# Transposing the last four token tiles by DMA, and moving query projections and evacuations forward, in a fused adaLN transformer block

## The chip, the cores and the metric

The kernel runs on one core of one Trainium2 chip. The metric is the device time of one execution in microseconds (us); lower is better. Kernels are compared in the same rounds on the same chip.

The engines are called PE (matrix multiplies; PEld is its weight loads), ACT (activation functions), DVE (vector work), POOL, and SP, which here issues the DMA transfers.

## The reference, cut to what matters

```python
mod = (_silu(c) @ w_mod).reshape(c.shape[0], 6, 1, -1)       # shift, scale, gate, twice
h = _layernorm(x) * (1 + ca) + sa                            # x: 1 x 2048 x 1024
x = x + ga * _A_ref(h, wq, wk, wv, wo)   # 32 query heads of 32, ONE key and value head
h = _layernorm(x) * (1 + cb) + sb
x = x + gb * _B_ref(h, w1, w3, w2)       # silu(h@w1) * (h@w3) @ w2, F = 3584
```

There are 2048 tokens, so 16 token tiles of 128. A "head group" is four query heads; there are eight. Every head needs a softmax over 2048 x 2048 scores. Those exponentials are ACT's main work: 1024 instructions, which start 0.92 us apart (median) when they follow one another.

## The kernel before

The program does not issue its instructions by hand. It adds nodes to a graph, each with an engine, a modelled duration, a priority (`prio`, lower goes first) and, for PE, the PSUM banks that it may use. At build time a list scheduler turns the graph into a fixed order for each engine. The program then holds one list for each engine, with waits on semaphores in it. So a change of priorities is a change of five orders.

Query block 0 (256 queries) starts while the first norm is still running, so this head of the kernel has much to arrange:

```python
def tr(t0, nt, allow=None):              # four token tiles: 32 PE transposes, 8 copies out of PSUM
    G.chain = 3
    ln_transpose(nt, t0, lambda c: HT[:, c, t0 * P:(t0 + nt) * P], ..., EV[t0 // 4], ...)
    G.chain = 0
...
def vproj(tb, allow=None):               # values of 512 tokens: 32 products of 128 x 32
    def vmm(e, b, i):
        tt, c = i // NC, i % NC
        return e.matmul(b[:, tt * 32:(tt + 1) * 32], HT[:, c, tb * 512 + tt * P:tb * 512 + (tt + 1) * P],
                        WKS[:, 1, c, :], start=c == 0, stop=c == NC - 1)
    ...
# the head, in the order in which the nodes are added
kproj(0, 256, (2, 3, 4, 5, 6, 7))        # keys; banks 2 to 7 are those of the scores
qproj(0, 256, 0, (2, 3, 4, 5, 6, 7), prio=1)
kproj(256, 256, (2, 3, 4, 5, 6, 7))
kproj(512, 512, (1,))
...
qproj(0, 256, 1, (0, 1))                 # queries of head group 1
vproj(0, (0, 1))
vproj(1, (0, 1))
for f in range(2, HEAD):
    qproj(0, 256, f, (0, 1))
tr(8, 4, (0, 1))
for t in range(12, 16):
    ln(t)
kproj(1024, 512, (0, 1))
tr(12, 4, (0, 1))
kproj(1536, 512, (0, 1))
for tb in range(2, NTB):
    vproj(tb, (0, 1))
...
wo_load = dma(lambda e: e.dma_start(WO[:], wo_in.rearrange("(c p) f -> p c f", p=P)), "wo", writes=["WO"],
              clear=[("WQR", k) for k in range(3)], nbytes=D * D * 2, after=xl)     # 2 MB
...
def warm(b, k):                          # PE work without a use, meant to hold the clock up (e5 and e6 test it)
    def f(e):
        for _ in range(k):
            r = e.matmul(PB[b][:, 0:P], IDENT[:], IDENT[:], start=True, stop=True, skip_group_check=True)
```

A score group is eight PE products that write the score banks; two exponentials on ACT read them.

The softmax here doesn't subtract the row's maximum and nothing guards it: scores larger than these inputs give would overflow.

## Time and profile before

| what | value | view |
|---|---|---|
| time | 1160.13 us, median of 3 (1158.57 to 1160.46) | runs |
| span of the profiled execution | 1158.1 us | page |
| busy PE, ACT | 97%, 89% | page |
| first and last exponential start | 29.2 and 1046.6 us | timeline |
| start of the last exponential to the end | 111.5 us, nearly PE alone | timeline |
| ACT waits for scores, 26 to 110 us | 11.7 us, longest 5.6 | waits |

From the first exponential to the last, ACT and PE are both nearly full. An exponential that starts 1 us earlier is worth up to 1 us, if nothing takes it back later and if the PE work left after the last exponential doesn't grow. So two quantities are followed below: the *lead* (how much earlier the n-th exponential starts than in the kernel before) and the *tail* (from the start of the last exponential to the end).

The page of the kernel before. The first line is the span, then the granted PE clock in tenths for 40 equal slices (29 us each), then two of the DMA queues.

```profile
span 1158.1 us, 35702 instructions
...
PEclk8899999999989999999999999999999999999999
...
q1 hardware_dynamic: 383184, 208.69, 64.5%
q8 instruction: 125, 2.05, 0.8%
```

The waits of the kernel before: ACT from 26 to 110 us, then one line of PE's from 20 to 110 us. Columns: total us, how often, longest.

```profile
engine line waited for: us in total, times, longest us
ACT UREG L925 <- PE SP L915: 11.7, 9, 5.6
...
PE PB L637 <- issue: 1.4, 1, 1.4
```

The timeline of the kernel before around its longest ACT wait. Columns: start, duration, engine, line, operation, tiles, count, and in brackets the idle time before it and what ended it.

```profile
57.75 0.37 SPq L813 DMA_DIRECT2D WO<-in_A_wo_dram  x1
...
59.67 1.05 PE L658 MATMUL PB<-HREG,WREG 128*128 128x256 bf16 x8
...
60.76 0.48 DVE L661 TENSOR_SCALAR QT<-PB,BIA 128x256 bf16<-128x256 f32 x1 [0.22 <-PE PB L658]
61.41 0.40 PE L915 MATMUL SP<-QT,KT 32*128 32x256 bf16 x8
...
61.86 14.38 ACT L925 ACTIVATE UREG<-SP 128x1024 bf16<-128x1024 f32 x15 [5.57 <-PE SP L915]
```

The fourth head group's query projection ran at 59.67 us, behind transposes and value products. Its scores at 61.41 us ended 5.57 us of ACT's idleness. The change aims at this wait.

The table by stretches of the kernel before. After the length come each engine's busy us, then the granted PE clock, the share of the DMA engines' time, and GB/s.

```profile
core 0: us, PE busy (x) PEld busy (x) DVE busy (x) ACT busy (x) POOL busy (x), PEclk, DMA share, GB/s
...
18.00:26.00 8.00, 7.41 (x132) 6.45 (x132) 2.55 (x5) 5.25 (x11) 0.42 (x1) 0.57 1.07 369
...
40.00:50.00 10.00, 8.42 (x156) 5.31 (x160) 8.31 (x27) 7.95 (x10) 4.89 (x12) 0.71 0.29 84
50.00:60.00 10.00, 8.40 (x203) 6.60 (x204) 7.97 (x25) 6.30 (x7) 0.18 (x1) 1.00 0.47 123
60.00:70.00 10.00, 10.00 (x194) 5.82 (x192) 3.64 (x9) 8.03 (x9) 0.00 (x0) 1.00 0.98 335
...
320.00:340.00 20.00, 11.53 (x232) 5.73 (x225) 15.55 (x26) 18.81 (x21) 1.70 (x2) 0.74 0.50 131
```

The clock fell twice in the head (0.57 and 0.71), and PE lost 8.5 of 20 us in a hole near 320 us.

### The profile page before, as it was taken

The page shows a single profiled execution, that of the slowest core. Times are in us where ns is not written, and L with a number is a line of the kernel's source. Part 1 is how long each engine was busy: PE and PEld are TensorE (multiplying, and loading weights), DVE is VectorE, ACT ScalarE, POOL GpSimd, SP SyncE. Part 2 cuts the span into 40 slices and gives each one's busy share as a digit, 9 for nine tenths or more (in the row PEclk, how much of TensorE's full clock was granted, in tenths as well). Part 3 has the DMA queues.
Part 4 walks back from the last instruction along what each step waited for, and adds up shares of the span by engine and source line. Part 5 has one row for each costly group of instructions (what it writes and reads, how often), then busy time and mean ns, then how long its engine had stood idle before and what let it go on. Part 6 is the DMA issues. An engine that isn't in the chain of part 4 may idle for free.

```text
span 1158.1 us, 35702 instructions
## 1 busy us (share of the span) xinstructions
PE 1122.6 (97%) x15918; PEld 767.1 (66%) x15918; DVE 984.7 (85%) x1498; ACT 1027.6 (89%) x1170; POOL 43.5 (4%) x86
## 2 busy tenths in 40 slices
PE   7799998999979999999999999999999999999998
PEld 6564444776646766777577766776677766777887
DVE  5837889999888999899999998999989999997452
ACT  5789999999999999999999999999999999992110
POOL 3200001000000001000100001000100010000000
PEclk8899999999989999999999999999999999999999
DMA  9337005956546565856496567766586649756996
GB/s 331 113 129 220 19 2 127 275 169 178 166 122 190 169 193 149 248 170 192 119 279 196 159 177 194 226 169 174 152 252 181 185 122 258 204 152 192 284 291 160
DMA packets 385417, 211.10 MB, mean 182 GB/s; under 512 B 21744, under 2 KB 376048, under 8 KB 385264
## 3 DMA queue, kind: packets, MB, share of 16 engines
q1 hardware_dynamic: 383184, 208.69, 64.5%
q8 instruction: 125, 2.05, 0.8%
q10 hardware_dynamic: 2080, 0.13, 0.1%
q14 instruction: 28, 0.23, 0.1%
HBM read 201.46 MB, written 4.19 MB: 178 GB/s over the span
## 4 chain that ended last, share of the span: by engine, by line
PE 92%; ACT 3%; DVE 3%; DMA 1%; SPq 1%; issue 0%; POOL 0%; DVEq 0%
PE PB L1141 33%; PE PB L1175 16%; PE SP L915 14%; PE PB L975 11%; PE PB L1107 5%; PE PB L658 4%; PE SP L1141 3%; ACT UREG L925 3%; PE SP L1175 2%; PE PB L1002 2%; DMA UREG<-in_w_mod_dram 1%; PE PB L637 1%; PE PB L838 0%; PE SP L1107 0%; DVE WO L850 0%
## 5 line engine op out<-in xcount | busy, mean ns | idle before, releaser
L925 ACT ACTIVATE UREG<-SP 128x1024 bf16<-128x1024 f32 x1024 | 968.6, 1075 | 18.8 <-PE SP L915 16.4
L948 DVE TENSOR_TENSOR UREG<-UREG 128x2048 bf16<-128x2048 bf16 x240 | 292.8, 1220 | 12.8 <-ACT UREG L925 10.8
L915 PE MATMUL SP<-QT,KT 32*128 32x256 bf16 x4096 | 204.8, 274 | 16.0 <-ACT UREG L925 15.0
L1141 PE MATMUL PB<-QT,WREG 128*128 128x256 bf16 x1648 | 207.4, 274 | 1.8 <-DVE DSB L1026 1.6
L1141 PEld LDWEIGHTS PB<-QT,WREG 128*128 128x128 bf16 x1648 | 150.1, 98 | 46.8 <-issue 31.2
L942 DVE TENSOR_TENSOR UREG<-UREG 128x2048 bf16<-128x2048 bf16 x120 | 146.4, 1220 | 11.5 <-PE PB L1002 6.4
L915 PEld LDWEIGHTS SP<-QT,KT 32*128 32x128 bf16 x4096 | 61.2, 93 | 138.6 <-ACT UREG L925 79.6
L1141 PE MATMUL PB<-QT,HREG 128*128 128x256 bf16 x1056 | 133.7, 274 | 0.8 <-DVE DSB L1026 0.8
L975 PE MATMUL PB<-UREG,V 128*32 128x256 bf16 x4032 | 132.2, 277 | 1.7 <-DVE QT L610 0.9
L975 PEld LDWEIGHTS PB<-UREG,V 128*32 128x32 bf16 x4032 | 99.3, 98 | 27.5 <-issue 17.9
L1141 PEld LDWEIGHTS PB<-QT,HREG 128*128 128x128 bf16 x1056 | 96.1, 98 | 29.7 <-issue 19.6
L1175 PE MATMUL PB<-WREG,HREG 128*128 128x256 bf16 x812 | 101.2, 273 | 0.0
L1175 PEld LDWEIGHTS PB<-WREG,HREG 128*128 128x128 bf16 x812 | 75.3, 98 | 20.4 <-issue 11.4
L1175 PE MATMUL PB<-HREG 128*128 128x256 bf16 x532 | 67.8, 274 | 0.0
L1141 PE MATMUL PB<-QT,X 128*128 128x256 bf16 x528 | 67.8, 274 | 0.0
L658 PE MATMUL PB<-HREG,WREG 128*128 128x512 bf16 (+1 forms) x312 | 64.1, 343 | 0.3 <-DVE DSB L1026 0.3
L957 DVE TENSOR_TENSOR UREG<-UREG 128x2048 bf16<-128x2048 bf16 x52 | 63.4, 1220 | 0.5
L1150 ACT ACTIVATE GSB<-GSB 128x512 bf16<-128x512 bf16 x56 | 38.8, 693 | 27.5 <-DVE GSB L1148 27.5
L1014 DVE COPY XN<-PB 128x256 f32<-128x256 f32 x63 | 26.6, 422 | 39.6 <-PE PB L1002 39.3
L1175 PEld LDWEIGHTS PB<-HREG 128*128 128x128 bf16 x532 | 49.2, 98 | 14.3 <-issue 8.0
L1107 PE MATMUL PB<-WO,QT 128*128 128x512 bf16 x232 | 57.6, 381 | 0.2 <-DVE QT L661 0.2
L1141 PEld LDWEIGHTS PB<-QT,X 128*128 128x128 bf16 x528 | 48.2, 98 | 14.3 <-issue 9.3
(139 smaller groups left out, 1031.9 us busy)
## 6 DMA issues: line engine op xcount, KB each, us to landing
WREG<-in_B_w_dram SPq DMA_DIRECT2D x112, 512.0 KB, 5.1
HREG<-in_B_w_dram SPq DMA_DIRECT2D x74, 512.0 KB, 5.2
WREG<-in_B_w_dram SPq DMA_DIRECT2D x33, 896.0 KB, 5.1
X<-in_B_w_dram SPq DMA_DIRECT2D x38, 512.0 KB, 5.1
HREG<-in_B_w_dram SPq DMA_DIRECT2D x21, 896.0 KB, 5.2
X<-in_B_w_dram SPq DMA_DIRECT2D x10, 896.0 KB, 5.1
X<-in_A_x_dram SPq DMA_DIRECT2D x32, 256.0 KB, 5.0
WREG<-in_w_mod_dram SPq DMA_DIRECT2D x16, 512.0 KB, 4.7
```

What stands on the lines that cost most here:

```text
L658: g = mm_group(NC, lambda e, b, c: e.matmul(b[:, 0:n], WQ[:, c, f * P:(f + 1) * P], HT[:, c, sl], start=c == 0, stop=c == NC - 1), lambda ...
L915: r = e.matmul(SP[:, b, o:o + qn], KT[32 * gg:32 * gg + 32, kts[j] * P:(kts[j] + 1) * P], QT[32 * gg:32 * gg + 32, f, q0:q0 + qn], start=T ...
L925: G.add("act", lambda e, u=u, h0=h0, n=n, b0=b0, nb=nb: e.activation(U[:, u, h0 * W:(h0 + n) * W].rearrange("p (b w) -> p b w", b=nb), SP[ ...
L942: G.add("dve", lambda e, tr=tr, u=u, fu=first_u: e.tensor_tensor(TR[:, tr, 0:4 * W], U[:, fu, 0:4 * W], U[:, u, 0:4 * W], ALU.add), reads= ...
L948: G.add("dve", lambda e, tr=tr, u=u: e.tensor_tensor(TR[:, tr, 0:4 * W], TR[:, tr, 0:4 * W], U[:, u, 0:4 * W], ALU.add), reads=[("TR", tr) ...
L957: G.add("dve", lambda e, ta=ta, tb=tb: e.tensor_tensor(TR[:, ta, 0:4 * W], TR[:, ta, 0:4 * W], TR[:, tb, 0:4 * W], ALU.add), reads=[("TR", ...
L975: r = e.matmul(PB[g.bank][32 * gg:32 * gg + 32, 0:qn], V[:, kt, :], U[:, pu, (gg * npk + j) * qn:(gg * npk + j + 1) * qn], start=w0 + n == ...
L1014: G.add("dve", lambda e, g=g, f=f: e.tensor_copy(ASB[:, f % 4, 0:qn], PB[g.bank][:, 0:qn]), writes=[("ASB", f % 4), ("XN", 2 + f % 4 // 2) ...
L1107: g = mm_group(NC, lambda e, b, f, t=t, h=h: e.matmul(b, QT[:, f, t * P:(t + 1) * P], WO[:, f, h * 512:(h + 1) * 512], start=f == 0, stop= ...
L1141: return e.matmul(b[:, j * qn:(j + 1) * qn], w13[:, w, c, j * P:(j + 1) * P], QT[:, c, q0:q0 + qn], start=c == 0, stop=c == NC - 1)
L1150: G.add("act", lambda e, b=b: e.activation(TB[b], GS[b], ACT.Tanh, scale=0.5), reads=[("GS", b)], writes=[("TB", b)], clear=alias("TB") if ...
L1175: G.add("pe", lambda e, g=g, j=j, fc=fc, hf=hf, first=first, w2s=w2s: e.matmul(PB[g.bank][:, j * 256:(j + 1) * 256], HHT[:, hf * NH + fc, ...
```

## The change

The intent was to take away ACT's waits in the head. Four query projections go ahead of values, evacuations of queries and values go ahead of norms on DVE, and the last four tiles (12 to 15) are transposed by DMA. The diff, cut to its core:

```diff
-              writes=[("V", tb)], groups=[(g, "r")], dur=dve_t(128), prio=1)
+              writes=[("V", tb)], groups=[(g, "r")], dur=dve_t(128), prio=-4)
...
-              writes=qkeys(f, t0, n), groups=[(g, "r")], dur=dve_t(n), prio=-5 if t0 == f == 0 else 1)
+              writes=qkeys(f, t0, n), groups=[(g, "r")], dur=dve_t(n), prio=-5 if t0 == 0 and f < HEAD else 1)
...
+    DMAT = range(12, 16)
-    EV = (("act",), ("act",), ("dve",), ("dve",))
+    EV = (("act",), ("act", "dve"), ("dve",), ("dve",))
...
+        if t in DMAT:
+            lastt[:] = [dma(lambda e: e.dma_start_transpose(HT[:, :, t * P:(t + 1) * P], xnt(t)), ("ht", t),
+                reads=[("XN", t)] + xnk(t), writes=[...], nbytes=P * D * 2 * 2)]
...
-    kproj(512, 512, (1,))
+    kproj(512, 512, (6, 7))
...
-    qproj(0, 256, 1, (0, 1))
+    qproj(0, 256, 1, (0, 1), prio=1)
     vproj(0, (0, 1))
+    qproj(0, 256, 2, (0, 1), prio=1)
     vproj(1, (0, 1))
-    for f in range(2, HEAD):
-        qproj(0, 256, f, (0, 1))
+    for f in range(3, HEAD):
+        qproj(0, 256, f, (0, 1), prio=1)
...
-                  clear=[("WQR", k) for k in range(3)], nbytes=D * D * 2, after=xl)
+                  clear=[("WQR", k) for k in range(3)], nbytes=D * D * 2, after=xl + lastt)
...
-                r = e.matmul(PB[b][:, 0:P], IDENT[:], IDENT[:], ...)                                      # warm-up, 128 wide
+                r = e.matmul(PB[b], IDENT[:], IDENT[:].unsqueeze(1).broadcast_to([P, 4, P]), ...)         # 512 wide
-    G.warm = (WARM, P / 2400.0 + 0.0026, warm, ident)
+    G.warm = (WARM, MM, warm, ident, 26.0)
```

More of the change, by code (lines that the diff above doesn't have):

```diff
@@ L227, in schedule @@
             if e == "pe" and self.warm is not None and t < self.warm[0]:
-                gap = s - t_free[e] - 0.3 - (0.1 if mode != "F" else 0.0) - (0.1 if n.mode != "F" else 0.0)
+                gap = s - t_free[e] - (0.05 if t < self.warm[4] else 0.3) - (0.1 if mode != "F" else 0.0) - (0.1 if n.mode != "F" else 0.0)
                 fb = [x for x in free_banks() if x[0] + SEM_LAT <= t_free[e]]
@@ L524, in build @@
             writes=[("QT", a, S - 512 + b) for b in range(0, 512, P)], dur=0.6)
-    htk = lambda c, t0, n: [("HT", c, i) for i in range(t0 // 256, (t0 + n) // 256)]
+    htk = lambda c, t0, n: [("HT", c, i) for i in range(t0 // P, (t0 + n) // P)]
     def ln_stats(t, s=None, bp=0):
@@ L678, in ln @@
     def ln(t):
-        (ln_stats_act if t in ONACT else ln_stats)(t)
+        bp = -3 if t >= 8 else 0
+        if t in ONACT:
+            ln_stats_act(t)
+        else:
+            ln_stats(t, bp=bp)
         ln_scale(t, 1)
-        ln_norm(t, t, en="pool" if t in ONPOOL else "dve")
+        ln_norm(t, t, en="pool" if t in ONPOOL else "dve", bp=bp)
+        if t in DMAT:
+            lastt[:] = [dma(lambda e: e.dma_start_transpose(HT[:, :, t * P:(t + 1) * P], xnt(t)), ("ht", t),
+                reads=[("XN", t)] + xnk(t), writes=[k for c in range(NC) for k in htk(c, t * P, P)], nbytes=P * D * 2 * 2)]
     def tr(t0, nt, allow=None):
@@ L689, in build @@
     prev = []
+    lastt = []
     done_ln = 0
@@ L788, in build @@
     G.chain = 0
-    kproj(0, 256, (2, 3, 4, 5, 6, 7))
-    qproj(0, 256, 0, (2, 3, 4, 5, 6, 7), prio=1)
-    kproj(256, 256, (2, 3, 4, 5, 6, 7))
-    kproj(512, 512, (1,))
+    kproj(0, 256, (2, 3, 4, 5))
+    qproj(0, 256, 0, (2, 3, 4, 5), prio=1)
+    kproj(256, 256, (6, 7))
+    kproj(512, 512, (6, 7))
     wscale(1, WVK)
@@ L795, in build @@
     bias(1, (0,), vb=True)
-    qproj(0, 256, 1, (0, 1))
+    qproj(0, 256, 1, (0, 1), prio=1)
     vproj(0, (0, 1))
+    qproj(0, 256, 2, (0, 1), prio=1)
     vproj(1, (0, 1))
-    for f in range(2, HEAD):
-        qproj(0, 256, f, (0, 1))
-    tr(8, 4, (0, 1))
+    for f in range(3, HEAD):
+        qproj(0, 256, f, (0, 1), prio=1)
+    if 8 not in DMAT:
+        tr(8, 4, (0, 1))
     for t in range(12, 16):
@@ L804, in build @@
     kproj(1024, 512, (0, 1))
-    tr(12, 4, (0, 1))
+    if 12 not in DMAT:
+        tr(12, 4, (0, 1))
     kproj(1536, 512, (0, 1))
@@ L1215, in f @@
             for _ in range(k):
-                r = e.matmul(PB[b][:, 0:P], IDENT[:], IDENT[:], start=True, stop=True, skip_group_check=True)
+                r = e.matmul(PB[b], IDENT[:], IDENT[:].unsqueeze(1).broadcast_to([P, 4, P]), start=True, stop=True, skip_group_check=True)
             return r
         return f
-    G.warm = (WARM, P / 2400.0 + 0.0026, warm, ident)
+    G.warm = (WARM, MM, warm, ident, 26.0)
     span = G.schedule(range(8))
```

## The prediction

> **What bounds the kernel now.** The page gives PE 97% and ACT 89% of 1158.1 us. The busy table by stretches: from the first exponential (29.2 us) until about 1048 us both engines are nearly full: exponentials saturate ACT and PE fills the gaps with feed-forward work. Then about 110 us are PE alone. By the waits, ACT idles only 18.8 us before exponentials, 11.7 of it between 26 and 110 us. Timeline: 2.56 us at 33.0 (third score group waits for the keys of tokens 512 to 1023), 0.76 and 1.29 us at 43 to 47, and 5.57 us at 56.3 to 61.9 (the fourth head group's query projection, evicted at 60.76, stands behind 64 transposes and two value products). A second hole, at 320 to 335 us, costs PE 8.5 us (scores alone; the next norm's second tile is late) but ACT little.
>
> **What the change does.** (a) It puts query projections 1 to 3 before the transposes and gives their evictions and the value evictions priority over norms. (b) Tiles 12 to 15 are transposed by DMA: 32 PE transposes (about 0.06 us each, 2 us) and 8 DVE copies (0.416 us each, 3.3 us) go; four DMA transposes come. The twelve existing ones land in 3.1 us (median; worst 7.0). (c) Four of eight ACT evictions of tiles 4 to 7 (0.6 us each) go to DVE, idle there (20.4 to 25.5 us). (d) Keys 512 to 1023 now use score banks, so in the instruction order the second score group comes behind that key projection, a query projection and half a value product. (e) Warm-up matmuls are 512 wide.
>
> **Critical path.** ACT's idle time in the head counts. The 5.57, 0.76 and 1.29 us should nearly go. (d) brings a new idle of 2.5 to 4 us before the second score group (about 31 to 34 us), in place of the 2.56. The transposes should be just in time, up to 1.5 us late. ACT saves about 6 to 8 us. But reading the instruction orders, PE is then behind relative to ACT: after the last score group about 3.5 us more PE work remains (each group at its traced duration). In return the 320 us hole mostly fills. An estimate that replays both orders for PE and ACT with durations from the trace (exponential 0.927 us, 256-column matmul 0.109, 512-column 0.216, score group 0.33) gives 6 us less.
>
> The granted clock was 0.5 from 18.6 to 25.4 and from 39 to 45.4 us. [...] The second dip should go (1 us); the first probably stays.
>
> **Prediction.** 1153 us, 8 in 10 between 1148 and 1158. Faster by over 2%: 0.02; within 2%: 0.97; slower: 0.01.
>
> **Signs.** Right: no ACT wait over 2 us between 40 and 70 us; the sixteenth score group some 7 us earlier; a 2 to 4 us ACT wait near 31 to 34 us; PE-only tail about 113 us; hole near 320 us under 4 us. Wrong: PE waiting at the key projection of tokens 1536 to 2047 for a DMA transpose; exponentials waiting on DVE-fed keys or queries.
>
> **What would make it wrong.** DMA transposes slow or queued; the first clock dip also gone (2 to 3 us more gain); a new late hole, as everything after the head is reordered.

1160.1 us, less 6 us by the replay and 1 us for the second clock dip, comes to the 1153 us.

## More of the kernel before

Line numbers differ: the exponential is L925 in the kernel before and L937 after; the score product is L915 and L927. The value projection is L648 in both.

The page calls queue 8 "instruction"; its 125 packets of 2.05 MB in all are 16 KB each. That they are PE's is read from the counts: the built program has 32115 instructions for PE, a product counted as two, or 257 to a packet (after the change 31864 and 124 packets, again 257).

## The result, and the profile after

| | before | after |
|---|---|---|
| median of 6 runs each, same rounds | 1159.47 us (1158.47 to 1160.46) | 1161.46 us (1160.48 to 1162.68) |
| ratio | | 1.0018, 95% interval 1.0005 to 1.0031 |
| span of the profiled execution | 1158.1 us | 1160.6 us |

Ratios are computed as the mean time of one kernel's fast runs over the mean time of the other's in the same rounds, so they are not quite the ratios of the medians quoted beside them. The kernel got very slightly slower; the prediction was 1153 us, with 1148 to 1158 as its range.

The page after:

```profile
span 1160.6 us, 35376 instructions
...
PEclk9989999999999999999999999999999999999999
...
q8 instruction: 124, 2.03, 0.7%
```

The waits after: ACT from 26 to 110 us, then two lines of PE from 20 to 110 us. "issue" is time in which PE waited for nothing that the profile shows.

```profile
engine line waited for: us in total, times, longest us
ACT UREG L937 <- PE SP L927: 10.9, 10, 3.9
...
PE PB L648 <- issue: 3.3, 1, 3.3
PE SP L637 <- issue: 1.1, 1, 1.1
```

ACT's total barely fell, from 11.7 to 10.9 us, but it is made of other waits. The timeline after shows which (first ACT's early part, then the stretch around 60 us):

```profile
27.45 1.91 ACT L937 ACTIVATE UREG<-SP 128x1024 bf16<-128x1024 f32 x2
33.25 15.75 ACT L937 ACTIVATE UREG<-SP 128x1024 bf16<-128x1024 f32 x17 [3.89 <-PE SP L927]
...
51.26 1.85 SPq L688 DMA_TRANSPOSE HREG<-GBB  x1
...
53.16 0.58 SPq L825 DMA_DIRECT2D WO<-in_A_wo_dram  x1
...
56.90 1.69 PE L637 MATMUL PB<-HREG,WKS 128*32 128x512 bf16 x28
...
59.19 1.25 PE L648 MATMUL PB<-WKS,HREG 128*128 128x32 bf16 x38
...
63.70 0.23 PE L648 MATMUL PB<-WKS,HREG 128*128 128x32 bf16 x2 [3.27 <-issue]
63.87 0.61 PE L927 MATMUL SP<-QT,KT 32*128 32x256 bf16 x8
64.41 0.82 PE L648 MATMUL PB<-WKS,HREG 128*128 128x32 bf16 x24
64.53 1.94 ACT L937 ACTIVATE UREG<-SP 128x1024 bf16<-128x1024 f32 x2 [3.61 <-PE SP L927]
```

The reader should see three things. First, the planned gain came: after 33.25 us ACT ran without a wait until 60.92 us, where the kernel before had waits of 0.76, 1.29 and 5.57 us. Second, the key projection that needs the DMA transposes (56.90 us) did not wait for them. Third, at 60.44 us PE stopped in the middle of the value products, after 38 of 64, with nothing to wait for, and stood still for 3.27 us. ACT ran out of scores and waited 3.61 us.

The table by stretches, after:

```profile
18.00:26.00 8.00, 7.64 (x192) 5.86 (x193) 4.99 (x15) 4.70 (x10) 0.18 (x1) 1.00 1.07 370
...
40.00:50.00 10.00, 7.60 (x132) 4.02 (x132) 9.11 (x27) 10.00 (x12) 2.42 (x7) 1.00 0.39 88
50.00:60.00 10.00, 9.99 (x264) 5.91 (x256) 4.09 (x9) 10.00 (x12) 0.00 (x0) 1.00 1.03 206
60.00:70.00 10.00, 6.73 (x133) 4.24 (x129) 0.72 (x4) 4.80 (x6) 0.00 (x0) 0.66 0.98 308
...
60.40:61.90 1.50, 0.03 (x2) 0.00 (x0) 0.08 (x1) 0.52 (x1) 0.00 (x0) 1.00 1.08 404
61.90:63.70 1.80, 0.00 (x0) 0.00 (x1) 0.00 (x0) 0.00 (x0) 0.00 (x0) 0.50 1.06 364
61.70:68.50 6.80, 4.80 (x77) 2.89 (x81) 0.29 (x1) 3.11 (x4) 0.00 (x0) 0.52 1.00 308
...
320.00:340.00 20.00, 17.54 (x290) 11.46 (x292) 17.95 (x28) 18.87 (x22) 1.70 (x2) 0.91 0.77 202
```

Both early clock dips are gone, and a new one has come with the stop: 0.52 from 61.7 to 68.5 us. PE stopped at 60.44 us and the granted clock was half (0.50) from 61.92 us, 1.5 us later, while PE still stood. During the half clock and just after it ACT waited again, 0.85 and 0.98 us. In the kernel before, the dip at 18.54 us followed a gap of 0.95 us (15.16 to 16.11 us) and began within one of 0.63 us, and the one at 39.02 us began together with a gap of 1.33 us.

The lead, from the start of the n-th exponential in each profile (minus: earlier than in the kernel before). The last three columns belong to experiments below.

```
exponential  before   after   e1_wo_wait  e3_pe_transposes  e11_pe_bank
     0        29.2    -1.76     -1.66         -1.42            -0.58
     4        35.6    -0.52     -0.38         +1.48            -1.12
    28        65.9    -8.76     -8.62         -6.88            -8.32
    32        69.5    -4.95     -8.48         -6.89            -8.33
    36        73.4    -3.11     -8.36         -6.06            -7.48
   128       162.5    -2.92     -8.20         -7.07            -8.51
   176       210.2    -1.06     -6.42         -6.13            -7.57
  1023      1046.6    -1.25     -6.65         -6.04            -7.51
```

So the sum of the profiled execution is: 8.76 us of lead at the 29th exponential; 5.65 us lost by the 37th, to the stop and the half clock after it; 1.86 us lost after that, nearly all between the 129th and the 177th; 1.25 us left at the last exponential. The tail is 115.2 us instead of 111.5, 3.7 us longer. 3.7 minus 1.25 is the 2.5 us by which the span grew.

### Why PE had no instructions

The trace records each 16 KB packet on queue 8. I counted PE's instructions in the built programs, a product as two (weight load and multiply) and a separate wait as one. The 18 profiles hold 22 PE waits of 0.95 us or more between 20 and 110 us that the profile calls "issue". Every one of them ends at position 706, 962, 963, 1986, 1987 or 2242. All of these leave 194 or 195 when divided by 256, whatever the order of the kernel. Long stops with a shown releaser lie elsewhere (in the kernel before at remainders 168 and 170). So in these profiles PE stops at the borders of blocks of 256 instructions.

With these borders one can read, for each block, when PE entered it, when the fetch that brings the next one began, and when the next one's first product ran. Which packet brings which block is my reading of their order; the trace doesn't name it. In the kernel after, the second packet began at 26.06 us and the stop at position 706, the third border, ended at 28.58 us; the seventh began at 61.27 us and the stop at 1986, the eighth border, ended at 63.70 us. An excerpt:

```
kernel              PE enters  next block's   so the fetch  next block   PE stood
                    block at   fetch begins   was late by   runs at      still
before                62.61       65.68          3.07          68.01        -
after                 55.27       61.27          5.99          63.70       3.27
a1_after_again        57.13       62.90          5.77          65.36       3.08
e13_early_2           56.92       62.08          5.16          64.43       2.35
e4_key_bank           56.18       59.94          3.76          62.38       1.0
e1_wo_wait            55.42       56.18          0.76          60.42        -
e2_wo_quarters        57.29       58.80          1.51          62.29        -
e3_pe_transposes      58.51       59.74          1.23          64.45        -
```

In the kernel before, at the 37 borders with the DMA engines under 30% busy, a fetch began at most 1.83 us after PE entered the block ahead of the one that it brings (0.41, 0.26 and 0.04 us at three borders of the head). Where PE stood still in this table, the new block ran 2.35 to 2.46 us after its fetch began. In the kernel after, the block between 55.27 and 60.44 us lasted only 5.17 us, because value products are short (76 instructions in 1.25 us). The fetch was late by 5.99 us. 5.99 + 2.43 - 5.17 is 3.25 us, the stop.

The load of `wo` was in flight then: issued at 53.16 us, landed 12.4 us later, with the DMA engines' share at 1.0 in that stretch. The trace also lists the load's own packets, 1024 of 2 KB. The first started at 54.43 us, 0.84 us before PE entered the block, and 885 of them had started when the fetch began. Packets of the loads issued behind it started only from 61.01 us on, so the fetch was kept back while this load was moved, not those. In the kernel before it was issued at 57.75 us, 0.2 us after one fetch (57.54 us), and the next fetch was late by 3.07 us in a block of 5.4 us; PE escaped by a hair.

### The profile page after: what moved, and what is told of

It is laid out like the page before. It is cut to its first block, busy times and chain, and to the rows that moved or that the text cites. A ratio compares the mean times of both kernels' runs of the same rounds, so it can differ in the third digit from the quotient of the medians.

```text
span 1160.6 us, 35376 instructions
## 1 busy us (share of the span) xinstructions
PE 1122.4 (97%) x15796; PEld 761.0 (66%) x15796; DVE 988.0 (85%) x1494; ACT 1024.8 (88%) x1166; POOL 38.1 (3%) x86
## 4 chain that ended last, share of the span: by engine, by line
PE 58%; ACT 35%; DVE 5%; issue 1%; DMA 0%; POOL 0%; SPq 0%
ACT UREG L937 32%; PE PB L1187 13%; PE PB L1153 11%; PE SP L927 8%; PE PB L987 6%; PE PB L1119 4%; PE PB L658 4%; PE SP L1187 4%; PE SP L1153 3%; ACT GSB L1162 1%; ACT WREG L1162 1%; PE PB L1014 1%; DVE UREG L960 1%; DVE UREG L954 1%; PE PB L850 1%
## 5 line engine op out<-in xcount | busy, mean ns | idle before, releaser
L960 DVE TENSOR_TENSOR UREG<-UREG 128x2048 bf16<-128x2048 bf16 x240 | 292.1, 1217 | 12.4 <-ACT UREG L937 10.5
L987 PE MATMUL PB<-UREG,V 128*32 128x256 bf16 x4096 | 129.2, 274 | 0.9 <-ACT UREG L937 0.5
L1187 PE MATMUL PB<-WREG,HREG 128*128 128x256 bf16 x728 | 92.6, 273 | 1.7 <-DVE HREG L1165 1.3
L1187 PEld LDWEIGHTS PB<-WREG,HREG 128*128 128x128 bf16 x728 | 66.7, 98 | 23.2 <-issue 13.9
L1187 PE MATMUL PB<-HREG 128*128 128x256 bf16 x448 | 57.3, 273 | 1.3 <-DVE HREG L1165 1.3
L1162 ACT ACTIVATE WREG<-WREG 128x512 bf16<-128x512 bf16 x56 | 39.7, 710 | 20.5 <-DVE WREG L1160 20.5
L1187 PEld LDWEIGHTS PB<-HREG 128*128 128x128 bf16 x448 | 41.0, 98 | 14.4 <-issue 9.2
```

What stands on the lines that cost most here:

```text
L960: G.add("dve", lambda e, tr=tr, u=u: e.tensor_tensor(TR[:, tr, 0:4 * W], TR[:, tr, 0:4 * W], U[:, u, 0:4 * W], ALU.add), reads=[("TR", tr) ...
L987: r = e.matmul(PB[g.bank][32 * gg:32 * gg + 32, 0:qn], V[:, kt, :], U[:, pu, (gg * npk + j) * qn:(gg * npk + j + 1) * qn], start=w0 + n == ...
L1162: G.add("act", lambda e, b=b: e.activation(TB[b], GS[b], ACT.Tanh, scale=0.5), reads=[("GS", b)], writes=[("TB", b)], clear=alias("TB") if ...
L1187: G.add("pe", lambda e, g=g, j=j, fc=fc, hf=hf, first=first, w2s=w2s: e.matmul(PB[g.bank][:, j * 256:(j + 1) * 256], HHT[:, hf * NH + fc, ...
```

## The experiments

**Theory A**: the `wo` load, moved by the change to just before PE enters a dense block, delays the fetch, and that stop costs nearly the whole gain. **Rival B**: the DMA transposes are to blame themselves, by delivering late or by crowding the DMA engines. The expectations below name further rivals in their own words. Two more suspects are parts of the change: the keys of tokens 512 to 1023 in score banks, and the new warm-up matmuls. All outputs are right.

| run | median us (range) | ratio to before | 95% interval | stop near 60 us |
|---|---|---|---|---|
| a1_after_again | 1163.26 (1161.85 to 1168.01) | 1.0035 | 1.0020 to 1.0049 | 3.1 us |
| e1_wo_wait | 1157.48 (1157.01 to 1160.91) | 0.9982 | 0.9970 to 0.9994 | none |
| e2_wo_quarters | 1158.68 (1157.24 to 1159.35) | 0.9983 | 0.9971 to 0.9995 | none |
| e3_pe_transposes | 1156.11 (1154.94 to 1158.91) | 0.9971 | 0.9958 to 0.9983 | none |
| e4_key_bank | 1159.70 (1157.66 to 1163.52) | 0.9995 | 0.9981 to 1.0010 | 1.0 us |
| e5_old_warm | 1163.11 (1160.70 to 1163.72) | 1.0019 | 1.0007 to 1.0031 | none in its profile |
| e6_before_warm | 1160.34 (1159.18 to 1161.73) | 1.0000 | 0.9987 to 1.0013 | none |
| e8_wait_bank | 1157.78 (1156.23 to 1158.07) | 0.9977 | 0.9964 to 0.9989 | none |
| e9_before_late | 1159.80 (1158.04 to 1161.60) | 1.0000 | 0.9988 to 1.0012 | none |
| e10_wo_later | 1159.61 (1156.90 to 1161.51) | 0.9998 | 0.9984 to 1.0011 | none in its profile |
| e11_pe_bank | 1155.49 (1155.02 to 1156.23) | 0.9957 | 0.9944 to 0.9969 | none |
| e12_wo_first | 1164.42 (1161.41 to 1165.28) | 1.0030 | 1.0018 to 1.0043 | 1.7 us, at 70 us |
| e13_early_2 | 1162.96 (1160.37 to 1166.74) | 1.0019 | 1.0002 to 1.0035 | 2.4 us |
| e14_early_4 | 1158.99 (1156.95 to 1160.01) | 0.9990 | 0.9975 to 1.0005 | none |

### The kernel after, again

> The changed kernel again, unedited, on one chip with the next three, to have its spread beside theirs. Theory A: the PE gap in the value projections (3.3 us at 60.4 us) is there again, because the load and the fetch meet at the same place in every run; ratio to the kernel before 1.000 to 1.003. If the gap was an accident of one profiled run, it is gone and the ratio is below 0.999.

The stop came again, at the same instruction:

```profile
61.04 1.25 PE L648 MATMUL PB<-WKS,HREG 128*128 128x32 bf16 x38
65.36 0.23 PE L648 MATMUL PB<-WKS,HREG 128*128 128x32 bf16 x2 [3.08 <-issue]
```

It comes 2 us later because of an earlier border: at 27 us PE stood for 1.6 us by "issue" (1.1 in the first profile), and the clock was then 0.57 from 30 to 34 us (1.00 in the first profile), so that the second score group came 1.9 us later. That accounts for 2 us between these two executions of one kernel. It comes and goes: of the 15 profiles with a stop at position 706 (1.1 to 1.6 us), 8 show a half clock of 3.4 us soon after it and 7 do not. So leads should be compared only between profiles of the same kind: after, e1 and e11 have none, a1, e2 and e3 have one.

### e1_wo_wait: one more wait before the load

The load gets one more wait, for the eviction of the last value projection. The orders of all five engines stay as they are. The loads behind this one in SP's list are held back too: the next one was issued at 62.44 us, against 53.78 in the kernel after.

```diff
         vproj(tb, (0, 1))
+    G.last_v = G.last_write[("V", NTB - 1)]
...
+    wo_load.extra = [G.last_v]          # SP waits for it before it issues the load
     span = G.schedule(range(8))
```

> The changed kernel with one wait added: the 2 MB load of the output weights is issued only after the last value projection is evicted (about 60.5 us instead of 53.2). All five instruction orders stay as in the changed kernel. Theory A (PE starves for instructions at 60.4 us because its 16 KB instruction fetch, seen at 61.27 us, 463 PE instructions after the one before, queues behind that load): the fetch comes before 60 us, the 3.3 us PE gap in the value projections shrinks below 1 us, ACT's 3.6 us wait there and the two waits after it at half clock go, lead over the kernel before at the 32nd exponential about 8.5 us instead of 5.0, time about 1156.5 us. Rival B (the DMA transposes' data come late and hold PE): gap stays about 3.3 us at the same matmul, time about 1161.5. Rival C (the lost time was coming anyway from later stages): gap goes, but time stays within 1 us of 1161.5.

```profile
59.33 1.29 PE L653 MATMUL PB<-WKS,HREG 128*128 128x32 bf16 x40
60.56 0.40 PE L933 MATMUL SP<-QT,KT 32*128 32x256 bf16 x8
60.89 0.76 PE L653 MATMUL PB<-WKS,HREG 128*128 128x32 bf16 x24
...
62.01 0.38 SPq L831 DMA_DIRECT2D WO<-in_A_wo_dram  x1
```

The value products (L653 here) now run through: 40, the score group, 24. The fetch began at 56.18 us, 0.76 us after PE entered the block. The lead at the 37th exponential is 8.36 us, against 3.11. So the moment of the load, with the same instructions in the same order, is worth 5.3 us there. Theory A holds and B cannot explain it, since the transposes are untouched. The loads that moved along are not a rival: in the kernel after their packets started only 0.26 us before the late fetch. The time is 0.18% below the kernel before. That is less than the prediction's 6 us, so a second, smaller error remains; it is taken up below.

### e2_wo_quarters: the same load in four parts

```diff
+        for i in range(4):
+            r = e.dma_start(WO[:, i * k:(i + 1) * k, :], wo_in[i * k * P:(i + 1) * k * P, :]...)
+            if i < 4 - 1:
+                r.then_inc(sem, 16)
+                e.wait_ge(sem, 16 * (i + 1))     # a quarter is issued when the one before it has landed
```

> The changed kernel with the same 2 MB load at the same moment (53.2 us), in four pieces of 512 KB, each issued when the one before has landed, so that the queue ahead of an instruction fetch is never over 512 KB from it. Theory A (the fetch waits behind what is queued): the PE gap at 60 us is below 1.5 us, fetches come at most about 330 PE instructions apart there, time about 1156.5 to 1158 us. A weaker form A2 (any traffic at this time, not what is queued, starves the fetch): gap stays about 3 us. Rival B (transposes late): gap stays 3.3 us, time about 1161.5.

The fetch was late by 1.51 us, and no stop followed. The load begins at its old place, but never are more than 512 KB of it queued (and the loads behind it wait until 66.98 us). The fetch began when 255 of the first quarter's 256 packets had started. So here it is not the moment alone that does the harm, but how much is queued ahead of the fetch: with the whole load queued it was late by 5.99 us.

### e13_early_2 and e14_early_4: a part of the load earlier

512 KB, and in e14 1 MB, are issued with the first DMA transpose (near 46 us). The rest is issued at the old place.

```diff
+    wo_load = dma(lambda e: e.dma_start(WO[:, 2:, :], wo_in[2 * P:, :]...), "wo", ...)     # e14: 4 in place of 2
+    def early(e):
+        e.dma_start(WO[:, 0:2, :], wo_in[0:2 * P, :]...).then_inc(...)
+        return t12_fn(e)
```

> The changed kernel with a quarter of the output weights (512 KB) loaded before the first DMA transpose, the other 1.5 MB at the old moment (53.2 us). PE, ACT, DVE orders unchanged. Theory A (the fetch waits for what this load has queued): 512 KB less is about 1.5 us less at 350 GB/s (the load's own rate in the trace), so the PE gap in the value projections shrinks from 3.1 to 3.3 us to about 1.2 to 2.2 us; lead at the 32nd exponential grows by about that. Rival (all or nothing, or any load there): gap stays 3 us or vanishes for both sizes.

> As early_2 with half of the output weights (1 MB) loaded early and 1 MB at 53.2 us. Theory A: the fetch comes about 3 us earlier than in the changed kernel, at or before 58.5 us, so the gap is gone (under 0.5 us); time near the added wait's, ratio 0.998 to 0.999. If the early megabyte delays the first DMA transposes so that PE waits for keys, a wait for a DMA shows at the key projection instead.

With 1.5 MB at the old place the fetch was late by 5.16 us and PE stood for 2.35 us, more than was expected. With 1 MB it was late by 0.64 us and there was no stop. But e14 is no smaller dose of the same thing, and its expectation came true by luck: its load was issued at 56.80 us, its first packets started at 58.06 us, and the fetch, due at 57.54 us, began at 58.19 us, when 16 of 512 packets had started. In e13 the packets started 0.45 us before PE entered the block. So these two runs do not show how the delay grows with the size. The profiled run of e13 was also its slowest (1166.74 us, with further clock dips after 100 us), so only its stretch up to 65 us is used here.

### e10_wo_later: a load one block later

The wait of e1, but for the keys of tokens 1024 to 1535, so that the load is issued at 55.40 us.

```diff
+    G.last_v = G.last_write[("KT", 4)]
     kproj(1536, 512, (0, 1))
...
+    wo_load.extra = [G.last_v]
```

> The changed kernel with one wait: the output-weight load is issued only when the key projection of tokens 1024 to 1535 is evicted (about 55.3 us instead of 53.2), so 2 us later but, unlike the helpful wait, still ahead of the instruction fetch that came at 56.18 us when nothing was in its way. All five orders stay as in the changed kernel. Theory A (the fetch is served when that load is over): the PE gap in the value projections grows by the delay, from 3.2 to about 5 us, ending at 65.5 to 66.5 us; the fetch comes at about 63.3 to 65 us; time 1 to 3 us above the changed kernel's (ratio to before 1.004 to 1.005). Rival (a later load merely interferes less): gap 3 us or less, ratio 1.002 or less.

This missed: the profile shows no stop. The fetch began at 55.77 us and slipped in ahead of the load's packets, which started at 56.46 us. The next one was late by 3.05 us, and its block ran at 66.22 us, 2.77 us after the fetch began. In the stops above a new block needed 2.35 to 2.46 us, so this was a margin of some 0.3 us. But three of its five executions were 2.7 to 4.6 us longer than the profiled one, at clock 0.991 instead of 0.994. To catch one of those the same kernel was looked at twice more:

> A second look at wo_later. Its five executions spread over 4.6 us. Theory A with a race: the fetch, due at about 55.8 us, either slips ahead of the load issued at 55.4 us (no gap, about 1157 us, clock 0.994) or comes when the load is over (gap of 4 to 6 us at 60 us, about 1161 us, clock 0.991). An execution at about 1161 must show the gap; one at about 1157 must not.

> A third look at wo_later, the same expectation: gap and about 1161 us, or no gap and about 1157 us.

They took 1156.42 and 1158.62 us (state unknown), neither with a stop near 60 us. In the second the next fetch was late by 3.74 us and its block ran 2.43 us after it, with no margin left (PE stood for 0.28 us). That second profile also has the half clock near 31 us, worth 1.9 us at the 5th exponential, and the first has not. So a part of the spread can come from there; whether the slow executions of e10 hold a stop stays open.

### e9_before_late: the kernel before, with its load moved

```diff
+    G.last_v = G.last_write[("QT", HEAD - 1, 0)]
     tr(8, 4, (0, 1))
...
+    wo_load.extra = [G.last_v]
```

> The kernel before with nothing but one wait added: its output-weight load is issued when the fourth head group's query projection is evicted (about 61.3 us instead of 57.75). In the kernel before an instruction fetch came at 65.68 us, when that load was ending, 348 PE instructions after the one ahead of it, and PE just escaped. Theory A: the fetch now comes only at about 69 us, a PE gap of 1.5 to 4 us appears at 66 to 71 us, ACT waits 1.5 us or more there, and the time grows by 1 to 3 us (ratio 1.001 to 1.003). Rivals B and C (fetches have nothing to do with the load): no gap, ratio 0.999 to 1.0005.

This missed too. No stop appeared, because the fetch (61.62 us) again came just in time: the load's first packets started at 61.56 us, and 8 of 1024 had started. The next was late by 3.33 us, but its block lasted 6.9 us. Here a load did no harm where a fetch had just begun. The condition is narrower than "a load near a dense block": in the profiles of after, a1, e4 and e13, which have the stop near 60 us, the load's packets started 0.45 to 1.5 us before PE entered the block; in those of e10 and e14 they started 0.5 to 1.1 us after it, and in e9 0.06 us before the fetch.

### e3_pe_transposes: no DMA transposes

```diff
-    DMAT = range(12, 16)
+    DMAT = ()
```

> The changed kernel with tiles 12 to 15 transposed by PE again, all else of the change kept. In its order the load of the output weights no longer stands behind the DMA transposes, so it is issued when the last query weights are scaled (about 41.5 us) and is over by about 50 us. Theory A: no PE gap over 1.5 us at 55 to 70 us; PE has 32 transposes more (2 us), which ACT's lead hides; lead at the 32nd exponential 7 to 8.5 us; time about 1157 to 1158 us, so that the DMA transposes are to blame only through the moment of that load. Rival B' (the change's other parts brought the loss): the gap or another wait of 3 us or more stays between 55 and 70 us, time 1160 or more.

With nothing to stand behind, the load is issued near 43 us, and it has landed before the dense block. No stop, and 0.29% faster than the kernel before. The DMA transposes were thus not needed for the gain. By itself this run would fit B as well; e1 tells the two apart.

### e12_wo_first: DMA transposes, but the load not behind them

```diff
-                  clear=[("WQR", k) for k in range(3)], nbytes=D * D * 2, after=xl + lastt)
+                  clear=[("WQR", k) for k in range(3)], nbytes=D * D * 2, after=xl)
```

> The changed kernel with the DMA transposes kept and only the order between them and the output-weight load undone (it no longer has to follow the last of them), so that it is issued at about 41.5 us. Theory A: no PE gap from a late fetch at 60 us. The transposes now share the queue with 2 MB of that load and 1 MB of modulation weights, so they land later than the 3.2 to 4.7 us after issue seen in the changed kernel; if the last two land after about 57 us, PE waits for them at the key projection of tokens 1536 to 2047 (up to 3 us). Time between the added wait's and the changed kernel's: ratio 0.997 to 1.000.

This missed the other way: 1.0030. The load went out at 43.26 us, ahead of the transposes, and those now became late. The last was issued at 57.55 us instead of 51.26, and PE waited 0.9 us for one. The stop moved to the border at 70 us (fetch late by 3.19 us, 1.7 us lost). The load of `wo` had been moved by 54.6 us, so other loads were in that fetch's way. So the transposes and this load do get in each other's way. In this run B's mechanism is real; in the kernel after it is not what costs.

### e4_key_bank and e8_wait_bank: keys back in bank 1

```diff
-    kproj(512, 512, (6, 7))
+    kproj(512, 512, (1,))
```

> The changed kernel with the key projection of tokens 512 to 1023 back in a bank that scores do not use, as in the kernel before (one argument). Theory: the 3.9 us ACT wait at 29.4 to 33.3 us becomes two waits of together 2 to 2.5 us, because the second score group no longer waits for that bank; the lead at the 8th exponential grows by 1.5 us. Whether the gap at 60 us stays depends on how many PE instructions lie before it, as the scheduler reorders this stretch: if it stays, time 1160 to 1161; if it goes, about 1155.5. Rival (the score bank is not what holds the second score group): ACT wait stays 3.9 us.

> Both edits in one: the added wait before the output-weight load and the key projection out of the score banks. The key bank gave 1.4 us at the 4th exponential and nothing at the 24th when alone (8.7 against 8.55 us of lead). So expected: no gap at 60 us, lead at the 32nd exponential 8.5 us, about as fast as the added wait alone (ratio 0.997 to 0.9985). If the early 1.4 us is kept to the end, ratio near 0.9965.

In e4 the wait before the second score group fell from 3.89 to 1.31 us. The lead at the 5th exponential rose from 0.5 to 1.9 us. But at the 25th it was 8.7 us against 8.55, so waits in between had taken it. e8 is e4 with the wait of e1; 0.9977 against 0.9982 for e1 is within the intervals. This wait was predicted rightly, and beside the wait of e1 its removal gave nothing that can be told from noise.

### e5_old_warm and e6_before_warm: the warm-ups alone

e5 is the kernel after with the 128-wide warm-ups. e6 is the kernel before with the 512-wide ones. A second part of the warm-ups goes with the width, also in the change itself: how long a gap must be to be filled (0.3 us in the kernel before, 0.05 us in the first 26 us after).

```diff
-                gap = s - t_free[e] - (0.05 if t < self.warm[4] else 0.3) - ...
+                gap = s - t_free[e] - 0.3 - ...
...
-                r = e.matmul(PB[b], IDENT[:], IDENT[:].unsqueeze(1).broadcast_to([P, 4, P]), ...)
+                r = e.matmul(PB[b][:, 0:P], IDENT[:], IDENT[:], ...)       # e5; e6 does the reverse to the kernel before
```

> The changed kernel with the warm-up matmuls of the kernel before (128 wide, threshold 0.3). Other engines' orders are the same, PE differs in warm-ups alone. Theory: the wide warm-ups are what kept the clock full at 18.6 to 25.4 us; with the old ones the clock halves there again, first exponential at about 29.2 instead of 27.5 us, time 1.5 to 2 us longer (about 1163) if nothing else moves. As there are about 90 more PE instructions ahead, instruction fetches fall elsewhere, so the gap at 60 us may change. Rival (the first dip's absence was chance, or comes of something else in the change): clock stays full, first exponential at 27.5.

> The kernel before with only the warm-up matmuls of the change (512 wide, threshold 0.05 in the first 26 us). Theory: the clock stays full from 18.6 to 25.4 us, the first exponential comes at 27.4 instead of 29.2 us. As later waits (a query projection behind transposes) take up some of that, 0.5 to 1.8 us are left at the end: ratio 0.9985 to 0.9995. Rival (the wide warm-ups are not the cause of the missing dip): clock halves as before, first exponential at 29.2, ratio 1.000.

The stretch from 20 to 26 us, first of e5, then of e6:

```profile
20.00:26.00 6.00, 6.00 (x102) 5.20 (x103) 1.95 (x7) 2.64 (x6) 0.00 (x0) 0.50 1.07 362
```

```profile
20.00:26.00 6.00, 5.13 (x152) 4.07 (x149) 1.01 (x4) 3.59 (x8) 0.00 (x0) 1.00 1.07 362
```

The warm-ups alone decide the first clock dip, in both directions (0.50 in e5, 1.00 in e6); their width and the gap that they fill were not tried apart. With the old ones the first exponential starts at 29.39 us, as before (29.2); with the new ones the kernel after starts it at 27.45. In the kernel before, the new ones brought it only 0.57 us forward (PE then waited 0.7 us for modulation weights), and later waits took that back.

### e11_pe_bank: what the experiments point to

PE transposes (e3) and keys in bank 1 (e4), on the kernel after:

```diff
-    DMAT = range(12, 16)
+    DMAT = ()
...
-    kproj(512, 512, (6, 7))
+    kproj(512, 512, (1,))
```

> PE transposes for tiles 12 to 15 again, and the key projection of tokens 512 to 1023 out of the score banks. From the two runs of each part: no gap at 55 to 70 us, lead at the 4th exponential about 2 us, at the 32nd 7 to 9 us; ratio 0.996 to 0.9975. If the parts add up to the end, 0.996; if the second is absorbed as it was beside the wait, 0.997.

The waits of e11, ACT from 26 to 110 us:

```profile
ACT UREG L937 <- PE SP L927: 5.0, 10, 1.2
```

1155.49 us, 0.43% below the kernel before: the best, and better than both kernels. Its lead at the last exponential is 7.51 us and its tail that of the kernel after. Against e3 (0.9971) the keys in bank 1 may add something here, but the intervals overlap.

## Why the prediction was wrong

- **The 5.57, 0.76 and 1.29 us waits go: right.** ACT ran from 33.25 to 60.92 us without a wait. The sixteenth score group was to come 7 us earlier; its first exponential, the 31st, came 8.70 us earlier.
- **A new wait of 2.5 to 4 us before the second score group: right**, 3.89 us; but e4 shows that it hardly mattered.
- **DMA transposes just in time: right.** They landed in 3.2 to 4.7 us and the keys did not wait.
- **About 3.5 us more PE work in the tail: right**, 3.7 us. **The hole at 320 us mostly fills: right**: PE was idle 2.5 of 20 us there instead of 8.5.
- **The second clock dip goes: right. "The first probably stays": wrong**; it went, for 1.8 us at the first exponential. The prediction itself named this as a possible gain. e5 and e6 show the cause.
- **"No ACT wait over 2 us between 40 and 70 us": wrong**, and this is the step that failed. The prediction said "ACT saves about 6 to 8 us" and replayed both orders with waits for data alone. That saving was reached (8.76 us), but it did not last: PE ran out of instructions at 60.44 us, and the stop with the half clock after it took 5.65 us back by the 37th exponential. e1 shows the cause: with the load moved and all orders as they were, 5.3 of those 5.65 us are kept. In the sum, 6 us less was forecast and the profile shows 2.5 us more; 5.4 of these 8.5 us are the difference between the profiles of after and e1.
- **The rest of the sum was too large as well.** Even e1 gained only 2.9 us in its profile (6.65 of lead at the end, less 3.7 of tail), not 6. The replay must have carried 9.5 us of lead to the end (6 us net and 3.5 us of tail). In the profiles of after and e1 about 1.8 us of lead go between the 129th and the 177th exponential. There PE waits 1.8 us once for a DVE evacuation and the clock falls for some microseconds (0.91 from 190 to 210 us). This is read from the traces only; no run tests it.

A hint stood in the profile before and was not used: a PE wait of 1.4 us ended by "issue" (from 31.6 us on), at the border at position 963. A second one was in the diff: a 2 MB load got a new place in SP's list.

What stays open: how the DMA engines choose between the packets of a load and a waiting fetch (late by 5.99 us behind one load, by 1.51 us behind the same load in quarters), and how the delay grows with what is queued, as e14 did not test it; what makes the clock fall (it was half from 1.5, 2.0 and 1.8 us after PE stopped in after, a1 and e13, but only 8 of the 15 stops at position 706 were followed by it); whether the slow executions of e10 had a stop; and the loss near 185 to 210 us.

## What to carry to other kernels

When a change moves a large load, look at where PE's instruction blocks lie. In after, a1 and e13 PE went through one block of 256 instructions, many of them short products, in about 5.2 us, while the fetch of the next was late by 5.16 to 5.99 us with 1.5 to 2 MB of a load just ahead of it; PE then stood for 2.35 to 3.27 us. Treat an "issue" gap on a busy PE as a question about instruction supply (here all 22 such waits of 0.95 us or more lay at block borders): compare its position with the block borders and see what was queued on DMA when the fetch should have begun. And try to split a load that has time (e2: late by 1.51 us, no stop), or to issue it just after a fetch (the kernel before and e10: no stop in the profile), rather than all at once just ahead of one.
